# A cached attention head loop with a gated FFN beside it: FFN weights behind the heads, another split of K between VectorE and ScalarE

## The chip, the core and the metric

The kernel runs on one core of one Trainium2 chip. The metric is the device time of one execution in microseconds, as the median over runs. A profile of one execution lies beside it; its times are those of that execution.

## What is computed

One token is decoded. With `xn` the layer norm of `x` (1 x 576), the output is `x + attention(xn) + ffn(xn)`, all in float32:

```python
q = (xn @ wq).reshape(H=32, Dh=128)
scores = einsum("hd,hkd->hk", q, k_cache) * Dh**-0.5     # Sk = 16384 cached keys a head
o = einsum("hk,hkd->hd", softmax(scores), v_cache)
attention = o.reshape(4096) @ wo                          # 4096 -> 576
ffn = (gelu(xn @ w_gate) * (xn @ w_up)) @ w_down          # 576 -> 4608 -> 576
```

The K and V caches are 32 x 16384 x 128 numbers each. Every weight and cache element is read from HBM once: 587.6 MB in all.

## The kernel before

**Slots.** All large loads go through one pool of three SBUF tiles, `slots` (128 partitions x 64 KB). `slot()` takes them in turn; a load into a slot waits until everything that used the slot's last tile is done. Every large load is issued by SyncE (`load`, L60), in program order, so a load that waits holds back those behind it. A K or V load of a head is 8.4 MB, 64 KB a partition: one whole slot.

**Front.** The first slot is `mix`: the last 64 rows of wq, and for gate and up the fourth row of each partition with the last 64 rows. The second is wq. `project` (L121) multiplies the normalized x with a weight on TensorE, four groups of 32 output partitions at a time, and accumulates the steps in PSUM. Q for head h is spread over the partitions by `q_spread` (L143). `ffn` (L153) runs for gate and then up: three more rows of the weight into a new slot, one load each, then the projection, a ScalarE copy into the free end of the same slot (L162), and four small GpSimd copies that lay the result out over 128 partitions in `gu` (L164). So the slot is in use until those copies have landed. `ffn_act` (L171) makes `hT` from `gu` on DVE and ScalarE (tanh).

**Heads.** For each of the 32 heads K and V are loaded (L238, L239). `qk` (L192) works through K in eight blocks of 16 rows a partition: DVE multiplies the block with q in place (L198), ScalarE sums the last 6 rows of each block, one instruction a row with an accumulator that is read by a second instruction (L201), and DVE reduces the other 10 (L202). `softmax` (L204) takes the maximum over all partitions by way of TensorE (L206 to L212) and the exponential on ScalarE (L216). `pv` (L218) multiplies the probabilities with V: 32 matmuls (64 records in the profile) into one PSUM bank, of which only four masked strips are wanted. `out_a` (L225) masks and reduces that bank on DVE (L227, L229), `out_b` (L231) sums it over the partitions on TensorE; for head h - 1 both stand behind block 3 of head h.

**End.** wd (36 rows of 576 numbers a partition) is loaded in pieces of 28 and 8 rows, then wo (32 rows) in pieces of 20, 6, 3, 2 and 1. `add_out` (L255) multiplies one such row with one column of `hT` or `oT`, in two halves; even and odd rows go to different strips of the PSUM tile `acc`. At row `MERGE` of the last weight the two strips are added (L303, L305), and the rows after it go to one strip. Then x is added and the result stored (L309, L310).

The framework places the instructions of one engine in an order of its own where it is not told to keep the program's; the order used here is that of the built program.

Of the kernel before, what the change touches and what calls it, by code (L numbers as in the profile page):

```python
# [10 lines left out]
ALU = mybir.AluOpType  # L11
AX = mybir.AxisListType

P = 128
H, SK, DH = 32, 16384, 128
# [1 line left out]
R = SK // P  # L17
SUB = 16
NSUB = R // SUB
N_ACT = 6  # L20
SLOTS = 3
DJ = 4
DM = P * DJ
# [2 lines left out]
HALF = D // 2  # L26
HD = H * DH
QG, QB = HD // 4, 512
FG, FB = DF // 4, 384
WD_T = DF // P  # L30
WO_T = HD // P
WD_PIECES = (28, 8)
WO_PIECES = (20, 6, 3, 2, 1)
MERGE = 26


@with_exitstack
def kernel(ctx: ExitStack, tc: tile.TileContext, x, k_cache, v_cache, wq, wo, wg, wu, wd, out):
# [18 lines left out]
    def slot():  # L57
        return slots.tile([P, R * DH], F32, tag="s", name="slot")

    def load(dst, src):  # L60
        nc.sync.dma_start(dst, src)
        return dst

    mix, wq_t = slot(), slot()
    at = 0

    def part_of_mix(src):
        nonlocal at
        n = src.shape[1]
        at += n  # L70
        return load(mix[:, at - n : at], src)

    ROW3 = 3 * DF
    tails = {"q": part_of_mix(wtail["q"])}
    load(wq_t, wmain["q"])
    row3 = {}
    for n in "gu":
        row3[n] = part_of_mix(wmain[n][:, ROW3:])
        tails[n] = part_of_mix(wtail[n])

    xrow = cpool.tile([1, D], F32, name="xrow")
    nc.scalar.dma_start(xrow, xf)
# [38 lines left out]
    def project(steps, group, size):  # L121
        pg = ps_big.tile([P, 3, 512], F32, tag="pb", name="pg")
        for k, (j, rhs) in enumerate(steps):
            for b in range(group // size):
                for q in range(4):
                    lo = q * group + b * size
                    if j < DJ:
                        lhs = xnb[:, j, :]
                    else:
                        lhs = xtb[:, q // 2, :]  # L130
                        lo = (q % 2) * group + b * size
                    nc.tensor.matmul(pg[32 * q : 32 * q + 32, b, :size], lhs, rhs[:, lo : lo + size],  # L132
                                     start=k == 0, stop=k == len(steps) - 1)
        return pg[:, : group // size, :size]

    steps = [(DJ, tails["q"])] + [(j, wq_t[:, j * HD : (j + 1) * HD]) for j in range(DJ)]
    pq = project(steps, QG, QB)
    qrow = cpool.tile([P, QG], F32, name="qrow")
    nc.scalar.activation(qrow.rearrange("p (b f) -> p b f", f=QB), pq, AF.Copy)
# [3 lines left out]
    def q_spread(h):  # L143
        r = 32 * (h // (H // 4))
        lo = h % (H // 4) * DH
        pq = ps_s.tile([P, 512], F32, tag="sm", name="pq")
        nc.tensor.matmul(pq[:, :DH], ones[r : r + 1, :], qrow[r : r + 1, lo : lo + DH], start=True, stop=True)  # L147
        Q[h] = spool.tile([P, 1, DH], F32, name="qs")
        nc.scalar.activation(Q[h][:, 0, :], pq[:, :DH], AF.Copy)

    gu = cpool.tile([P, 2, WD_T], F32, name="gu")

    def ffn(which):  # L153
        n = "gu"[which]
        t = slot()
        steps = [(3, row3[n]), (DJ, tails[n])]
        for j in range(DJ - 1):
            lo, hi = j * DF, (j + 1) * DF
            steps.append((j, load(t[:, lo:hi], wmain[n][:, lo:hi])))
        gc = t[:, ROW3 : ROW3 + FG]  # L160
        pg = project(steps, FG, FB)
        nc.scalar.activation(gc.rearrange("p (b f) -> p b f", f=FB), pg, AF.Copy)  # L162
        for q in range(4):
            nc.gpsimd.dma_start(gu[32 * q : 32 * q + 32, which, :], gc[32 * q : 32 * q + 1, :])  # L164

    ffn(0)
    ffn(1)

    hT = cpool.tile([P, WD_T], F32, name="hT")

    def ffn_act():  # L171
        g, u = gu[:, 0], gu[:, 1]
        t1 = cpool.tile([P, WD_T], F32, name="t1")
        nc.vector.tensor_mul(t1, g, g)  # L174
        nc.vector.tensor_scalar(t1, t1, 0.044715, 1.0, op0=ALU.mult, op1=ALU.add)
        nc.vector.tensor_mul(t1, t1, g)
        th = cpool.tile([P, WD_T], F32, name="th")
        nc.scalar.activation(th, t1, AF.Tanh, scale=0.7978845608028654)
        t2 = cpool.tile([P, WD_T], F32, name="t2")
        nc.vector.scalar_tensor_tensor(t2, th, 1.0, g, op0=ALU.add, op1=ALU.mult)  # L180
        nc.vector.scalar_tensor_tensor(hT, t2, 0.5, u, op0=ALU.mult, op1=ALU.mult)  # L181
# [10 lines left out]
    def qk(h, i):  # L192
        kt = KT[h].rearrange("p (n d) -> p n d", d=DH)
        if i == 0:
            S[h] = spool.tile([P, R], F32, name="s")
        lo, nv = i * SUB, SUB - N_ACT
        blk = kt[:, lo : lo + SUB, :]
        nc.vector.tensor_mul(blk, blk, Q[h].to_broadcast([P, SUB, DH]))  # L198
        for n in range(nv, SUB):
            jk = spool.tile([P, DH], F32, name="jk", bufs=1)  # L200
            nc.scalar.activation(jk, blk[:, n, :], AF.Copy, accum_out=S[h][:, lo + n : lo + n + 1])  # L201
        nc.vector.tensor_reduce(S[h][:, lo : lo + nv], blk[:, :nv, :], axis=AX.X, op=ALU.add)  # L202

    def softmax(h):  # L204
        pm = spool.tile([P, 1], F32, name="pm")
        nc.vector.reduce_max(pm, S[h], axis=AX.X)  # L206
        pt = ps_s.tile([P, 512], F32, tag="sm", name="pt")
        nc.tensor.transpose(pt[:1, :P], pm, ident)  # L208
        nm = spool.tile([1, 1], F32, name="nm")
        nc.vector.tensor_reduce(nm, pt[:1, :P], axis=AX.X, op=ALU.max, negate=True)  # L210
        pb = ps_s.tile([P, 512], F32, tag="sm", name="pb")
        nc.tensor.matmul(pb[:, :1], ones[:1, :], nm, start=True, stop=True)  # L212
        nb = spool.tile([P, 1], F32, name="nb")
        nc.scalar.activation(nb, pb[:, :1], AF.Copy, scale=SCALE)  # L214
        PE_[h] = spool.tile([P, R], F32, name="pe")
        nc.scalar.activation(PE_[h], S.pop(h), AF.Exp, bias=nb, scale=SCALE, accum_out=lsum[:, h : h + 1])  # L216
# [8 lines left out]
    def out_a(h):  # L225
        o4 = PO[h % 2].rearrange("p (r d) -> p r d", d=DH)
        tc.keep_in_program_order(nc.vector.tensor_mul(o4, o4, sel.unsqueeze(2).to_broadcast([P, 4, DH])))  # L227
        OM[h] = spool.tile([P, DH], F32, name="om")
        nc.vector.tensor_reduce(OM[h], o4.rearrange("p r d -> p d r"), axis=AX.X, op=ALU.add)  # L229

    def out_b(h):  # L231
        pc = ps_s.tile([P, 512], F32, tag="sm", name="pc")
        nc.tensor.matmul(pc[:, :1], OM.pop(h), ones[:, :1], start=True, stop=True)  # L233
        nc.scalar.activation(oall[:, h : h + 1], pc[:, :1], AF.Copy)  # L234

    q_spread(0)
    for h in range(H):
        KT[h] = load(slot(), kv[h])  # L238
        VT[h] = load(slot(), vv[h])  # L239
        for i in range(NSUB):  # L240
            qk(h, i)
            if h == 0 and i == 3:
                ffn_act()
            if h > 0 and i == 3:
                out_a(h - 1)
                out_b(h - 1)
        KT.pop(h)
        softmax(h)
        if h + 1 < H:
            q_spread(h + 1)  # L250
        pv(h)

    seen = set()
# [5 lines left out]
                             start=q not in seen, stop=last)  # L259
            seen.add(q)  # L260

    wd0, wd1, wo1 = slot(), slot(), slot()
    a, b = WD_PIECES
    n0 = WO_PIECES[0]
    load(wd0[:, : a * D], wdv[:, : a * D])
    load(wd1[:, : b * D], wdv[:, a * D :])
    load(wd1[:, b * D : (b + n0) * D], wov[:, : n0 * D])
    lo = n0
    for n in WO_PIECES[1:]:
        load(wo1[:, (lo - n0) * D : (lo + n - n0) * D], wov[:, lo * D : (lo + n) * D])  # L270
        lo += n
    wd_rows = [wd0[:, j * D : (j + 1) * D] for j in range(a)] + [wd1[:, j * D : (j + 1) * D] for j in range(b)]
    wo_rows = [wd1[:, (b + j) * D : (b + j + 1) * D] for j in range(n0)]
    wo_rows += [wo1[:, j * D : (j + 1) * D] for j in range(WO_T - n0)]

    out_a(H - 1)
    out_b(H - 1)
    pl = ps_s.tile([P, 512], F32, tag="sm", name="pl")
    nc.tensor.matmul(pl[:, :H], ones, lsum, start=True, stop=True)
    rl = cpool.tile([P, H], F32, name="rl")  # L280
# [7 lines left out]
    oT = cpool.tile([P, WO_T], F32, name="oT")  # L288
    nc.gpsimd.dma_start(oT, orow)

    for j, w in enumerate(wd_rows):
        add_out(j % 2, hT[:, j : j + 1], w)

    x2 = wo1[:, R * DH - 2 * HALF : R * DH - HALF]
    nc.vector.memset(x2, 0.0)
    for i in range(2):
        nc.gpsimd.dma_start(x2[32 * i : 32 * i + 1, :], xf[:, i * HALF : (i + 1) * HALF])
    part = wo1[:, R * DH - HALF :]
    nc.vector.memset(part, 0.0)

    for j, w in enumerate(wo_rows):
        if j == MERGE:
            nc.vector.tensor_copy(part[64:], acc[64:, :HALF])  # L303
            for i in range(2):
                nc.tensor.matmul(acc[32 * i : 32 * i + 1, :HALF], ident[:, 64 + 32 * i : 65 + 32 * i], part,  # L305
                                 start=False, stop=False)
        add_out(j % 2 if j < MERGE else 0, oT[:, j : j + 1], w, last=j in (MERGE - 1, WO_T - 1))

    nc.vector.tensor_add(x2[:64], x2[:64], acc[:64, :HALF])  # L309
    nc.sync.dma_start(of.rearrange("o (a f) -> (o a) f", a=2), x2[0:64:32, :])  # L310
# [28 lines left out]
```

## Time and profile before

| | before |
|---|---|
| median of 3 runs (lowest to highest) | 1394.77 us (1393.31 to 1395.02) |
| profiled execution: time, span | 1390.13 us, 1388.4 us |
| DMA | 588.31 MB in 12367 packets, mean 424 GB/s |
| busy share of the span: PE, DVE, ACT | 30%, 71%, 47% |
| one block's DVE multiply (L198), reduce (L202) | 2283 ns, 1477 ns |
| one ScalarE row: ACTIVATE, accumulator read (L201) | 309 ns, 186 ns |
| mean TensorE clock granted | 0.63 |

Times are in microseconds from the start of the span unless marked ns. A line such as `L198` is a line of the kernel before. "A <- B" in a wait means that A waited for B. Queue q1 carries the large loads, q0 the GpSimd copies, q8 and q14 the fetching of the engines' instructions. Beside the views the trace holds each DMA packet with its start, duration, size and queue, but not the DMA engine that moved it; the 4-byte packets at the end of each load are its completion writes.

### The profile page before, as it was taken

To read this page: it belongs to the slowest core of one execution; us is meant where nothing else is said; L and a number is where in the kernel's file an instruction comes from. 1 tells how busy PE (TensorE), PEld (TensorE's weight loads), DVE (VectorE), ACT (ScalarE), POOL (GpSimd) and SP (SyncE) were. 2 spreads that over 40 slices of the span, in tenths; PEclk is the share of its full clock that TensorE was granted. 3 is DMA by queue.
4 is the path that set the end of the run, shared out by engine and by line. 5 is a ranking of instruction groups with operands and counts; after the bars stand their busy time and mean duration, and the time that the engine had idled before them with its cause. 6 is when DMAs were issued, how large, how long until landed. Compare 5 with 4: busy or idle time off the path is not lost.

```text
span 1388.4 us, 10333 instructions
## 1 busy us (share of the span) xinstructions
PE 415.1 (30%) x2881; PEld 113.9 (8%) x2881; DVE 990.0 (71%) x668; ACT 653.6 (47%) x3240; POOL 6.3 (0%) x17
## 2 busy tenths in 40 slices
PE   4511323333332122333231123333321223232317
PEld 1100000000000000000000000000000000000002
DVE  1008888777777887777777887777778887777770
ACT  0105555545454555445445555454545554454450
POOL 0000000000000000000000000000000000000000
PEclk9855565565655556565655665656555565656559
DMA  9999999999999999999999999999999999999996
GB/s 400 431 416 427 439 433 431 435 429 443 427 424 448 423 429 435 423 424 429 431 429 418 433 425 420 431 427 422 427 422 429 434 429 427 427 422 422 424 412 296
DMA packets 12367, 588.31 MB, mean 424 GB/s; under 512 B 1667, under 2 KB 1685, under 8 KB 2070
## 3 DMA queue, kind: packets, MB, share of 16 engines
q1 hardware_dynamic: 11956, 587.60, 98.9%
q8 instruction: 22, 0.36, 0.1%
q14 instruction: 35, 0.29, 0.1%
q0 software_dynamic: 352, 0.06, 0.0%
q10 hardware_dynamic: 2, 0.00, 0.0%
HBM read 587.60 MB, written 0.00 MB: 423 GB/s over the span
## 4 chain that ended last, share of the span: by engine, by line
DMA 49%; DVE 34%; PE 13%; ACT 4%; issue 1%; SPq 0%; POOL 0%; DVEq 0%; ACTq 0%
DMA slot<-in_A_k_cache_dram 41%; DVE slot L198 20%; DVE s L202 11%; PE po L222 10%; DMA slot<-in_B_w_up_dram 3%; ACT jk L201 3%; DMA slot<-in_A_wo_dram 2%; DMA slot<-in_A_wq_dram 2%; DMA gu<-slot 1%; PE pg L132 1%; DVE po L227 1%; DVE om L229 1%; PE acc L258 1%; ACT pe L216 1%; PE pt L208 0%
## 5 line engine op out<-in xcount | busy, mean ns | idle before, releaser
L201 ACT ACTIVATE jk<-slot 128x128 f32<-128x128 f32 x1536 | 475.0, 309 | 552.1 <-DVE slot L198 509.7
L198 DVE TENSOR_TENSOR slot<-slot,qs 128x2048 f32<-128x2048 f32 x256 | 576.4, 2283 | 211.2 <-DMA slot<-in_A_k_cache_dram 211.2
L202 DVE TENSOR_REDUCE s<-slot 128x10 f32<-128x1280 f32 x256 | 370.2, 1477 | 1.1
L222 PE MATMUL po<-slot,pe 128*4 128x512 f32 x2048 | 294.0, 738 | 14.8 <-ACT pe L216 14.5
L201 ACT ACTIVATION_READ_ACCUMULATOR jk<-slot 128x1 f32 x1536 | 286.4, 186 | 0.0
L208 PE MATMUL pt<-ident,pm 128*1 128x128 f32 x32 | 11.9, 373 | 460.9 <-DVE pm L206 460.9
L233 PE MATMUL pc<-ones,om 128*128 128x1 f32 x64 | 18.6, 359 | 438.2 <-DVE om L229 438.2
L222 PEld LDWEIGHTS po<-slot,pe 128*4 128x4 f32 x2048 | 54.5, 98 | 233.8 <-issue 209.7
L233 PEld LDWEIGHTS pc<-ones,om 128*128 128x128 f32 x64 | 15.8, 308 | 467.9 <-DVE om L229 467.9
L174 DVE TENSOR_TENSOR t<-gu 128x36 f32<-128x36 f32 x1 | 0.2, 196 | 65.1 <-DMA gu<-slot 65.1
L132 PE MATMUL pg<-slot,xnb 128*32 128x384 f32 (+1 forms) x256 | 31.5, 643 | 32.6 <-DMA slot<-in_A_wq_dram 13.2
L208 PEld LDWEIGHTS pt<-ident,pm 128*1 128x1 f32 x32 | 2.5, 79 | 464.8 <-DVE pm L206 411.1
L206 DVE TENSOR_REDUCE pm<-s 128x1 f32<-128x128 f32 x32 | 9.1, 286 | 36.7 <-ACT jk L201 36.7
L214 ACT ACTIVATE nb<-pb 128x1 f32<-128x1 f32 x32 | 5.5, 171 | 57.6 <-PE pb L212 57.6
L227 DVE TENSOR_TENSOR po<-po,sel 128x512 f32<-128x512 f32 x32 | 22.0, 688 | 11.3 <-PE po L222 11.3
L147 PE MATMUL pq<-qrow,ones 1*128 1x128 f32 x64 | 24.9, 489 | 0.0
L212 PE MATMUL pb<-nm,ones 1*128 1x1 f32 x64 | 17.7, 343 | 14.8 <-DVE nm L210 14.8
L229 DVE TENSOR_REDUCE om<-po 128x128 f32<-128x512 f32 x32 | 21.8, 682 | 0.0
L181 DVE SCALAR_TENSOR_TENSOR hT<-t,gu 128x36 f32<-128x36 f32 x1 | 0.2, 197 | 28.3 <-DMA gu<-slot 28.3
L210 DVE TENSOR_REDUCE nm<-pt 1x1 f32<-1x128 f32 x32 | 8.9, 279 | 15.0 <-PE pt L208 15.0
L212 PEld LDWEIGHTS pb<-nm,ones 1*128 1x128 f32 x64 | 15.9, 306 | 23.3 <-issue 22.6
L234 ACT ACTIVATE oall<-pc 128x1 f32<-128x1 f32 x32 | 5.5, 171 | 22.6 <-PE pc L233 22.6
(61 smaller groups left out, 116.6 us busy)
## 6 DMA issues: line engine op xcount, KB each, us to landing
slot<-in_B_w_gate_dram SPq DMA_DIRECT2D x4, 2304.0 KB, 44.4
slot<-in_B_w_up_dram SPq DMA_DIRECT2D x4, 2304.0 KB, 35.2
slot<-in_B_w_down_dram SPq DMA_DIRECT2D x1, 8064.0 KB, 35.6
slot<-in_A_wo_dram SPq DMA_DIRECT2D x1, 5760.0 KB, 26.7
slot<-in_B_w_down_dram SPq DMA_DIRECT2D x1, 2304.0 KB, 13.1
slot<-in_A_wo_dram SPq DMA_DIRECT2D x1, 1728.0 KB
slot<-in_B_w_gate_dram SPq DMA_DIRECT2D x1, 1152.0 KB
slot<-in_B_w_up_dram SPq DMA_DIRECT2D x1, 1152.0 KB, 39.4
```

The source lines that it names most:

```text
L132: nc.tensor.matmul(pg[32 * q : 32 * q + 32, b, :size], lhs, rhs[:, lo : lo + size], start=k == 0, stop=k == len(steps) - 1)
L147: nc.tensor.matmul(pq[:, :DH], ones[r : r + 1, :], qrow[r : r + 1, lo : lo + DH], start=True, stop=True)
L198: nc.vector.tensor_mul(blk, blk, Q[h].to_broadcast([P, SUB, DH]))
L201: nc.scalar.activation(jk, blk[:, n, :], AF.Copy, accum_out=S[h][:, lo + n : lo + n + 1])
L202: nc.vector.tensor_reduce(S[h][:, lo : lo + nv], blk[:, :nv, :], axis=AX.X, op=ALU.add)
L208: nc.tensor.transpose(pt[:1, :P], pm, ident)
L212: nc.tensor.matmul(pb[:, :1], ones[:1, :], nm, start=True, stop=True)
L216: nc.scalar.activation(PE_[h], S.pop(h), AF.Exp, bias=nb, scale=SCALE, accum_out=lsum[:, h : h + 1])
L222: nc.tensor.matmul(PO[h % 2][q : q + 4, :], pe[:, k : k + 4], vt[:, k * DH : (k + 4) * DH], start=k < 16, stop=k >= R - 16)
L227: tc.keep_in_program_order(nc.vector.tensor_mul(o4, o4, sel.unsqueeze(2).to_broadcast([P, 4, DH])))
L229: nc.vector.tensor_reduce(OM[h], o4.rearrange("p r d -> p d r"), axis=AX.X, op=ALU.add)
L233: nc.tensor.matmul(pc[:, :1], OM.pop(h), ones[:, :1], start=True, stop=True)
```

## The change

Gate and up leave the front: the first two slots hold wq and its small rest alone, and K of head 0 follows at once in the third. Their loads, projections and `ffn_act` now stand behind the last head, in three slots: three gate rows; a mixed slot with the fourth gate row, the gate tail, the fourth up row, the up tail and the copied gate result; three up rows with the copied up result. Then come wo (28 and 4 rows) and wd (24, 6, 3, 2, 1) in place of wd and then wo; the merge stands at row 30 of wd. ScalarE sums 8 of 16 rows in blocks 0 to 6 of each K and 4 in block 7 (60 a head in place of 48). The masking and reduction of head h - 1 stand behind the softmax of head h; in the built program the one-column product of `out_b` stands behind the first PV matmul of head h, and the first gate matmuls stand ahead of the last head's `out_b`.

```diff
-N_ACT = 6
+N_ACT = (8,) * (NSUB - 1) + (4,)
...
-WD_PIECES = (28, 8)
-WO_PIECES = (20, 6, 3, 2, 1)
-MERGE = 26
+WO_PIECES = (28, 4)
+WD_PIECES = (24, 6, 3, 2, 1)
+MERGE = 30
...
-    mix, wq_t = slot(), slot()
...
+    wq_t, qt = slot(), slot()[:, :QS]
+    load(qt, wtail["q"])
     load(wq_t, wmain["q"])
...
-    def ffn(which):
...
+    def ffn():
+        g, mix, u = slot(), slot(), slot()
+
+        def row(t, at, n, j):
+            return j, load(t[:, at * DF : (at + 1) * DF], wmain[n][:, j * DF : (j + 1) * DF])
+
+        def tail(at, n):
+            return DJ, load(mix[:, at : at + DF // 2], wtail[n])
+
+        steps = [row(g, 0, "g", 0), row(g, 1, "g", 1), row(g, 2, "g", 2), row(mix, 0, "g", 3), tail(2 * DF, "g")]
+        finish(0, project(steps, FG, FB), mix)
+        steps = [row(mix, 1, "u", 3), tail(5 * DF // 2, "u"), row(u, 0, "u", 0), row(u, 1, "u", 1), row(u, 2, "u", 2)]
+        finish(1, project(steps, FG, FB), u)
+
+    def finish(which, pg, t):
+        gc = t[:, 3 * DF : 3 * DF + FG]
         nc.scalar.activation(gc.rearrange("p (b f) -> p b f", f=FB), pg, AF.Copy)
         for q in range(4):
             nc.gpsimd.dma_start(gu[32 * q : 32 * q + 32, which, :], gc[32 * q : 32 * q + 1, :])
-
-    ffn(0)
-    ffn(1)
...
-        lo, nv = i * SUB, SUB - N_ACT
+        lo, nv = i * SUB, SUB - N_ACT[i]
...
         for i in range(NSUB):
             qk(h, i)
-            if h == 0 and i == 3:
-                ffn_act()
-            if h > 0 and i == 3:
-                out_a(h - 1)
-                out_b(h - 1)
         KT.pop(h)
         softmax(h)
+        if h > 0:
+            out_a(h - 1)
         if h + 1 < H:
             q_spread(h + 1)
+        if h > 0:
+            out_b(h - 1)
         pv(h)
...
+    ffn()
+    ffn_act()
...
+    ta, tb, te = slot(), slot(), slot()
+    a, b = WO_PIECES
+    wo_rows = load_rows(ta, 0, wov, 0, a) + load_rows(tb, 0, wov, a, b)
+    wd_rows = load_rows(tb, b, wdv, 0, WD_PIECES[0])
+    lo = WD_PIECES[0]
+    for n in WD_PIECES[1:]:
+        wd_rows += load_rows(te, lo - WD_PIECES[0], wdv, lo, n)
+        lo += n
```

More of the change, by code (lines that the diff above doesn't have):

```diff
@@ L28 @@
 QG, QB = HD // 4, 512
+QS = HD // 2
 FG, FB = DF // 4, 384
@@ L62, in load @@
         return dst
-    mix, wq_t = slot(), slot()
[L65 to L74, printed above, removed]
+    wq_t, qt = slot(), slot()[:, :QS]
+    load(qt, wtail["q"])
     load(wq_t, wmain["q"])
[L76 to L79, printed above, removed]
     xrow = cpool.tile([1, D], F32, name="xrow")
@@ L134, in project @@
         return pg[:, : group // size, :size]
-    steps = [(DJ, tails["q"])] + [(j, wq_t[:, j * HD : (j + 1) * HD]) for j in range(DJ)]
+    steps = [(DJ, qt)] + [(j, wq_t[:, j * HD : (j + 1) * HD]) for j in range(DJ)]
     pq = project(steps, QG, QB)
@@ L151 @@
     gu = cpool.tile([P, 2, WD_T], F32, name="gu")
-    def ffn(which):
[L154 to L161, printed above, removed]
+    def ffn():
[10 more added lines that the diff above has]
+        gc = t[:, 3 * DF : 3 * DF + FG]
         nc.scalar.activation(gc.rearrange("p (b f) -> p b f", f=FB), pg, AF.Copy)
@@ L228, in out_a @@
         OM[h] = spool.tile([P, DH], F32, name="om")
-        nc.vector.tensor_reduce(OM[h], o4.rearrange("p r d -> p d r"), axis=AX.X, op=ALU.add)
+        tc.keep_in_program_order(nc.vector.tensor_reduce(OM[h], o4.rearrange("p r d -> p d r"), axis=AX.X, op=ALU.add))
     def out_b(h):
@@ L260, in add_out @@
             seen.add(q)
[L262 to L274, printed above, removed]
     out_a(H - 1)
@@ L289, with load_rows @@
     nc.gpsimd.dma_start(oT, orow)
-    for j, w in enumerate(wd_rows):
-        add_out(j % 2, hT[:, j : j + 1], w)
-    x2 = wo1[:, R * DH - 2 * HALF : R * DH - HALF]
+    ffn()
+    ffn_act()
+    def load_rows(t, at, src, lo, n):
+        load(t[:, at * D : (at + n) * D], src[:, lo * D : (lo + n) * D])
+        return [t[:, (at + j) * D : (at + j + 1) * D] for j in range(n)]
+    ta, tb, te = slot(), slot(), slot()
[6 more added lines that the diff above has]
+        lo += n
+    x2 = te[:, R * DH - 2 * HALF : R * DH - HALF]
     nc.vector.memset(x2, 0.0)
@@ L297 @@
         nc.gpsimd.dma_start(x2[32 * i : 32 * i + 1, :], xf[:, i * HALF : (i + 1) * HALF])
-    part = wo1[:, R * DH - HALF :]
+    part = te[:, R * DH - HALF :]
     nc.vector.memset(part, 0.0)
     for j, w in enumerate(wo_rows):
+        add_out(j % 2, oT[:, j : j + 1], w)
+    for j, w in enumerate(wd_rows):
         if j == MERGE:
@@ L306 @@
                                  start=False, stop=False)
-        add_out(j % 2 if j < MERGE else 0, oT[:, j : j + 1], w, last=j in (MERGE - 1, WO_T - 1))
+        add_out(j % 2 if j < MERGE else 0, hT[:, j : j + 1], w, last=j in (MERGE - 1, WD_T - 1))
     nc.vector.tensor_add(x2[:64], x2[:64], acc[:64, :HALF])
```

## The prediction

> **What bounds the kernel now.** I read the page's slices and queues first, then rates by stage, then the queue's own waits, then the end of the chain. The page:
>
> ```profile
> span 1388.4 us, 10333 instructions
> ...
> DMA  9999999999999999999999999999999999999996
> ...
> q1 hardware_dynamic: 11956, 587.60, 98.9%
> q8 instruction: 22, 0.36, 0.1%
> q14 instruction: 35, 0.29, 0.1%
> ```
>
> The DMA engines carry packets in every slice; DVE (71%) and ACT (47%) do not. Neither version changes the 587.60 MB, so only three things can move the time: the slowest DMA engine's work, idle time on that engine, and what follows its last byte. Rates by stage (columns: stretch, busy us of each engine, PE clock, DMA share, GB/s):
>
> ```profile
> 76.00:80.00 4.00, 3.77 (x24) 0.99 (x24) 0.00 (x0) 0.00 (x0) 0.00 (x0) 0.50 0.66 279
> 180.00:580.00 400.00, 112.12 (x710) 30.18 (x710) 315.55 (x206) 208.36 (x1041) 0.00 (x0) 0.61 1.00 432
> 580.00:980.00 400.00, 109.70 (x712) 28.60 (x712) 313.02 (x206) 204.92 (x1026) 0.00 (x0) 0.61 1.00 427
> ```
>
> The heads start at 432 GB/s and fall to 427. The trace's packets say why. Each load ends with one 4-byte completion write per engine, 16 in all. At the loads landing from 488.1 to 1315.3 us one write comes last, by 2.5 to 4 us behind the next, and its intervals are of two kinds: 19.35 us (eight 64 KB packets of 2.418 us) or about 20.05. The longer ones hold one of the 8192-byte packets of q14. Such a packet takes 0.309 us and the 64 KB packet after it 2.80 instead of 2.418: 0.69 us together. These fetches come every 128 ACT instructions (every 45.6 us from 435.9 to 1348.9; the kernel has 110.5 ACT instructions a head of 39.4 us), and there are 28 of them. So **one DMA engine carries all of ACT's instruction fetches, and it finishes every load last**. The other 15 run ahead of it until they wait for SP:
>
> ```profile
> SPq L61 <- DVE s L202: 832.8, 32, 28.6
> SPq L61 <- PE po L222: 363.5, 32, 12.2
> SPq L61 <- DMA gu<-slot: 65.3, 2, 36.9
> SPq L61 <- ACT jk L201: 34.9, 32, 1.1
> ```
>
> SP's waits look large, but the slowest engine's shorter interval is exactly its packets: it waits for none of these in the heads. The end of the chain (start, us, what):
>
> ```profile
> 1347.57 26.70 DMA slot<-in_A_wo_dram
> 1374.27 0.14 issue
> 1374.40 6.53 PE acc L258 x104
> 1380.93 0.02 issue
> 1380.96 0.47 DVE slot L303
> ...
> 1382.12 2.93 PE acc L258 x24
> ```
>
> After the 20-row piece of wo lands (1374.27) PE is the limit: 26 rows in 6.53 us, 0.25 a row, on a clock that is already full. The last small piece lands at 1382.04, by its completion write, and does not hold PE up.
>
> **The change, part by part.**
>
> *Sharing of the K blocks.* Before, from the cadence in the chain, a block costs DVE 2.20 (multiply) + 1.39 (10 rows) = 3.59 us. ACT's rows come every 0.433 us. Now DVE needs 2.20 + 0.8 x 1.39 = 3.31 and ACT 8 x 0.433 = 3.46: ACT becomes the longer one. A K tile is released after 2.28 + 7 x 3.46 + 4 x 0.433 = 28.2 us, where it was 31.35 (1315.85 to 1347.20): 3.1 us earlier. That issues the next V load earlier and lets the 15 fast engines run about 3 us further ahead, which is worth nothing while the slowest engine never waits. But ACT gets 12 more rows a head, each an ACTIVATE and a read of its accumulator: 24 x 32 = 768 instructions, 6 more fetches of 128. At 0.69 us each on the slowest engine: **+4.1 us**. Ends: 5 packets of 0.31 alone give 1.6; 7 at 0.76 give 5.3. I take the middle, since 0.69 repeats over the whole run.
>
> *PV mask.* The two DVE operations (0.69 + 0.68 us) go from block 3 to behind the maximum of the next head. They end some 2.5 us after the K tile's last reduce; DVE then waits for K anyway (211.2 us over 31 heads, 6.8 each, and now 3 more). PE's one-column product stands behind the first PV matmul and may hold it 0.5 us; V's slot is needed over 10 us later. Nothing. Without that cover it is 1.4 us a head.
>
> *Gate and up out of the front.* K0's load waited for a slot held by the small gu copies, issued at 73.62; u's last row was through on the first engines at 74.0. The drop to 279 GB/s shows the hole, and 64 KB packets at 74.6 took up to 3.46 us. The engine that later is slowest has writes at 74.3 and 95.0: 20.7 for 19.34, so 1.35 lost; at V1's issue (133.6) another 0.2. Now K0 is issued at once into a free slot; V0 waits until wq is projected (35.1 as before; K0 is through at about 43.5, so 7 us are left after the issue), K1's slot is free by then. **-1.5 us**; ends -0.3 (the gap alone) and -2.7 (all that the fast engines lost).
>
> *Gate and up behind the heads.* With L the landing of K31 on the slowest engine (1315.85 before): g's rows wait for V30 (about L+2, needed L+11 by the fastest engines). The mixed slot waits for K31 (L+28.2; the fastest engines stand about 3 us, the slowest needs it at L+36). u's rows wait for V31 (L+41, needed L+46). wo's 28 rows wait for g's projection (L+48, after PV; needed L+63). The next slot waits for g's gu copies (L+66; 63.2 to 73.47 = 10 us before), needed L+82. The last slot waits for u's gu copies: u lands L+69, one row 4.1, copy 1.1, then 21.0 us as before (81.78 to 102.8), so L+97 with the issue; needed L+101 by the first, L+107 by the slowest engine. POOL does them in order behind the oT copy, long done; ACT's tanh stands ahead of u's copy and waits for g's copies until L+66, covered. Nothing on the slowest engine, with 10 us to spare.
>
> *The tail.* The order ends with wd, and the big piece before the last four is 24 rows instead of 20: 4 x 0.25 = 1.0 us more PE behind it. And PE has been idle: wo's 32 rows are done by about L+98, the 24 rows of wd land about L+107. In the windows the PE clock fell after such pauses:
>
> ```profile
> 1362.00:1366.00 4.00, 3.61 (x37) 1.15 (x41) 0.82 (x4) 0.27 (x1) 1.56 (x3) 0.57 0.99 426
> 1374.00:1378.00 4.00, 3.60 (x60) 1.61 (x64) 0.00 (x0) 0.00 (x0) 0.00 (x0) 1.00 0.89 364
> ```
>
> Before, the idle time ahead of the last rows was 1.5 us and the clock stayed at 1.00. At 0.50 a row takes 0.48. PV bursts stayed slow for 4.1 us (1310.13) to 5.7 (1349.71), the wd rows for 2.7 (1362.71); half of that is lost: 1.35 to 2.85, I take 2.0, the 4.1 row, as its pause was also a cold one. **+3.0 us** with the four rows; ends 1.0 (clock still full) and 3.9. Behind it merge, six rows, addition and store are as before.
>
> Sum: +4.1 - 1.5 + 3.0 = **+5.6 us**. The profiled execution took 1390.13 (span 1388.4 and 1.7 around it), so 1395.7; the median of the runs shown is 4.6 above that execution, so **1400.4**. A change under 0.2% (2.8 us) can't be told from none here.
>
> **Rivals.** *Fetches cost nothing* (17%): if the six fetches fall on engines that run ahead, the sum is -1.5 + 3.0 = +1.5: 1396.3. For it: q14 is 0.1% of the engines' time. Against: the long intervals of the last engine hold its fetches. The Trainium skill ("Trainium Runtime: NRT & Kernel Launch", section on instruction fetch mechanics) says that the sequencer streams its blocks itself and that crossing one is "mostly hidden"; by that rule this rival's time would stand. It is hidden for ACT in this trace, but not for the DMA engine (0.69 us).
>
> *The earlier V issue pays* (11%, faster): SP's late issue starves also the slowest engine, and 3 us more lead ends that. If 427 and 426 GB/s from 580 to 1340 us went back to 432, 324 MB would take 750.3 instead of 760: -9.7 + 1.5 = -8.2, 1386.6. It decides if the last completion write of a load shows gaps in which its engine had nothing queued. For it: 432 falls to 427 just when the lead is used up. Against: 19.35 us is eight packets with no gap.
>
> *The last slot comes late* (7%): if u's gu copies take 42 us instead of 21, the last load is issued 10.8 us too late: 1411.2. It decides above some 31 us. Against: both groups before took 10 and 21 us.
>
> That the new sharing shortens nothing, because ACT becomes the longer engine, alters no time here, as K is released off the slowest engine's path.
>
> **How the numbers follow.** Forecast 65%; with all its lower ends at once (1.6 - 2.7 + 1.0 = -0.1) it gives 1394.7, with all its upper ones (5.3 - 0.3 + 3.9 = 8.9) 1403.7; then 17, 11 and 7. The range 1394.0 to 1404.5 adds 0.7 for the spread of the runs shown (1393.31 to 1395.02); it holds the first two cases and leaves out the last two. Faster 0.11; same 0.19 (the 17% for the most part, and the low end of the forecast); slower 0.70.
>
> **What would show it.** q14 with about 41 packets; the last landing about 2.6 us later; K released 28 us after landing; no drop near 76 us; the clock at 0.5 when wd's 24 rows start and 30 rows in 9 to 10 us. Wrong if q14 stays, if heads run at 432 throughout, if DMA drops near the last slot's issue, or if the clock is 1.0 there.

## The result, and the profile after

The changed kernel takes 1398.54 us in the median of 10 runs (1396.59 to 1399.01); the kernel before, on the same chip, 1394.64 (1391.74 to 1396.32). The ratio is 1.003, 95% interval [1.002, 1.004]: slower by 3.9 us, where +5.6 was predicted. The profiled executions differ more, 1397.76 against 1390.13: the one of before lies 4.5 us under the median of its kernel, the one of after 0.8 under. What is read from that pair has to add up to their own difference in span, 6.5 us, not to 3.9.

The page of after:

```profile
span 1394.9 us, 11109 instructions
...
DMA  9999999999999999999999999999999999999995
...
q1 hardware_dynamic: 11956, 587.60, 98.4%
q8 instruction: 22, 0.36, 0.1%
q14 instruction: 41, 0.34, 0.1%
```

The large loads (q1) and the fetches of q8 are unchanged; q14 has six packets more, as forecast. Rates by stage (stretch, busy us of PE, PEld, DVE, ACT and POOL, PE clock, DMA share, GB/s):

```profile
76.00:80.00 4.00, 3.42 (x20) 0.60 (x24) 0.00 (x0) 0.68 (x4) 0.00 (x0) 0.50 0.93 397
180.00:580.00 400.00, 117.84 (x710) 29.30 (x710) 296.27 (x205) 256.24 (x1275) 0.00 (x0) 0.63 1.00 431
580.00:980.00 400.00, 119.77 (x710) 28.19 (x710) 295.67 (x203) 255.74 (x1273) 0.00 (x0) 0.63 1.00 425
1376.00:1380.00 4.00, 1.52 (x16) 0.56 (x20) 0.00 (x0) 0.00 (x0) 0.00 (x0) 0.50 0.98 398
1380.00:1384.00 4.00, 4.00 (x60) 1.41 (x55) 0.00 (x0) 0.00 (x0) 0.00 (x0) 0.79 0.20 76
```

The drop to 279 GB/s near 76 us is gone (397). The heads lose 1 to 2 GB/s. In the last two rows the clock is 0.50 when the big piece of wd is worked on and full only some 3 us into it. SyncE's waits in its queue (us, times, longest) and the end of the chain (start, us, what):

```profile
SPq L62 <- DVE s L194: 809.6, 32, 36.7
SPq L62 <- PE po L214: 407.3, 32, 13.6
SPq L62 <- DMA gu<-slot: 38.8, 3, 20.5
SPq L62 <- ACT jk L193: 33.2, 32, 1.1
```

```profile
1338.58 39.76 DMA slot<-in_B_w_down_dram
1378.34 0.14 issue
1378.48 9.05 PE acc L249 x120
1387.53 0.02 issue
1387.55 0.47 DVE slot L296
1388.03 0.04 issue
1388.07 0.65 PE acc L298 x4
1388.72 2.94 PE acc L249 x24
```

The 6.5 us, followed by the completion writes of the slowest DMA engine: K of head 0 landed at 95.1 us before and lands at 43.9 now. That is 51.2 earlier, of which 49.65 are the packets of gate and up, now behind the heads: the front saves 1.6. From there to V of head 30 it was 1200.2 and is 1205.7: +5.5. From that V, with K and V of head 31 still to come, to the landing of the last big piece, it was 78.97 and is 128.74 - 49.65 = 79.09: +0.1. The rows behind that landing: 9.05 against 6.53 us: +2.5. Sum +6.5; merge, last rows and store are as they were.

The 5.5 can be taken apart. The trace does not name a packet's DMA engine, but the packets that end in the last completion write of V of head 30 can be followed back to K of head 0, as each starts within 0.02 us of the end of the one before. In both executions this chain of packets has no gap: 488 packets of 64 KB, and between them 26 fetches before and 32 now. The fetches, each with what the packet behind it takes over 2.418 us, come to 17.0 and 21.0 us, 0.65 each: +4.0. The rest is nearly all in other 64 KB packets that took over 2.45 us: their excess is 3.5 us before and 4.9 now.

### The profile page after: what moved, and what is told of

It is laid out like the page before. It is cut to its first block, busy times and chain, and to the rows that moved or that the text cites. A ratio compares the mean times of both kernels' runs of the same rounds, so it can differ in the third digit from the quotient of the medians.

```text
span 1394.9 us, 11109 instructions
## 1 busy us (share of the span) xinstructions
PE 442.6 (32%) x2881; PEld 113.9 (8%) x2881; DVE 939.3 (67%) x668; ACT 811.2 (58%) x4008; POOL 6.3 (0%) x17
## 4 chain that ended last, share of the span: by engine, by line
DMA 49%; ACT 28%; PE 16%; DVE 3%; issue 3%; POOL 0%; SPq 0%; DVEq 0%
DMA slot<-in_A_k_cache_dram 44%; ACT jk L193 27%; PE po L214 12%; DMA slot<-in_B_w_down_dram 3%; DVE slot L190 3%; DMA slot<-in_A_wq_dram 2%; PE pg L120 1%; PE acc L249 1%; DMA gu<-slot 1%; PE pc L225 1%; ACT pe L208 1%; PE pb L204 0%; PE pt L200 0%; DVE pm L198 0%; DVE nm L202 0%
## 5 line engine op out<-in xcount | busy, mean ns | idle before, releaser
L193 ACT ACTIVATE jk<-slot 128x128 f32<-128x128 f32 x1920 | 594.1, 309 | 331.6 <-DVE slot L190 272.1
L193 ACT ACTIVATION_READ_ACCUMULATOR jk<-slot 128x1 f32 x1920 | 357.4, 186 | 0.0
L214 PE MATMUL po<-slot,pe 128*4 128x512 f32 x2048 | 324.0, 692 | 16.2 <-ACT pe L208 16.2
L194 DVE TENSOR_REDUCE s<-slot 128x8 f32<-128x1024 f32 (+1 forms) x256 | 316.5, 1278 | 0.0
L204 PE MATMUL pb<-nm,ones 1*128 1x1 f32 x64 | 17.6, 342 | 14.8 <-DVE nm L202 14.8
L127 ACT ACTIVATE qrow<-pg 128x1024 f32<-128x1024 f32 x1 | 1.0, 1024 | 30.7 <-PE pg L120 30.7
```

Of the source, the lines that this page charges most:

```text
L214: nc.tensor.matmul(PO[h % 2][q : q + 4, :], pe[:, k : k + 4], vt[:, k * DH : (k + 4) * DH], start=k < 16, stop=k >= R - 16)
```

## Experiments

Two theories. The first is the prediction's: the heads last as long as one DMA engine needs, the one that carries ACT's instruction fetches at 0.69 us each, so the 12 extra ACT rows a head are what costs. The second: fetches cost little, and the rest does it, by the order at the end with its cold clock, by the moved masking, or by K released earlier. The table has the difference of each run's median to that of the kernel before on the same chip in the same series of runs; the ratio is taken over all their runs, so the two can differ by about a us.

| run | base | q14 packets | to before, us | ratio, 95% interval |
|---|---|---|---|---|
| after | | 41 | +3.9 | 1.003 [1.002, 1.004] |
| e1 new sharing alone | before | 41 | +4.7 | 1.0037 [1.0024, 1.005] |
| e2 more ACT instructions | before | 41 | +1.3 | 1.001 [0.9999, 1.0021] |
| e3 more DVE instructions | before | 41 | -3.2 | 0.9985 [0.9974, 0.9995] |
| e4 old sharing | after | 35 | -1.4 | 0.9992 [0.9984, 1.0001] |
| e5 wd in small pieces | after | 41 | +1.1 | 1.0004 [0.9994, 1.0013] |
| e6 two ACT rows | after | 19 | -13.3 | 0.99 [0.9888, 0.9912] |
| e7 two rows and small pieces | after | 19 | -15.4 | 0.9887 [0.9873, 0.99] |
| e8 masking moved alone | before | 35 | +1.0 | 1.0002 [0.9992, 1.0012] |
| e9 gate's slot freed in the front | before | 35 | -1.1 | 0.9993 [0.9983, 1.0002] |
| e10 K released late | after | 53 | +13.2 | 1.0096 [1.0082, 1.011] |
| e11 one ACT row, small pieces | after | 15 | -10.6 | 0.992 [0.9905, 0.9935] |
| e12 PE kept warm | after | 41 | +3.5 | 1.0023 [1.0014, 1.0032] |

**The sharing, alone and undone.** e1 puts only the new sharing into the kernel before; e4 takes only it out of the kernel after.

```diff
-N_ACT = 6
+N_ACT = (8,) * (NSUB - 1) + (4,)
...
-        lo, nv = i * SUB, SUB - N_ACT
+        lo, nv = i * SUB, SUB - N_ACT[i]
```

> The kernel before with the new split of K alone (8 ScalarE rows in blocks 0 to 6, 4 in block 7). Fetch theory: 768 more ScalarE instructions, 6 more q14 packets (41), the last load lands 4.1 us later (up to 5.4 if the restarts of the other engines add to it), nothing else moves: 1394.6 + 4.1 to 5.4 = 1398.7 to 1400.0. Rival, the heads go by when K's slot is freed: it is freed some 2 us earlier, so the time stays or falls, 1394.6 or less. Rival, the whole loss lies behind the last head: 1394.6.

```diff
-N_ACT = (8,) * (NSUB - 1) + (4,)
+N_ACT = (6,) * NSUB
```

> The changed kernel with 6 ScalarE rows in every block. Fetch theory: q14 back to 35 packets, the last load 4.1 to 5.4 us earlier than in the changed kernel, its end as slow as there: 1398.5 - 4.1 to 5.4 = 1393.1 to 1394.4; against the kernel before it shows the front (-1.5 forecast) and the end (+2.5) alone. Rival, the loss lies behind the last head: 1398.5. Rival, K's slot: freed 3 us later than in the changed kernel, 1398.5 or more.

e1 took 1398.93, +4.7. e4 took 1392.87, -1.4. The two add up (+4.7 - 1.4 = +3.3 for the +3.9 of the whole change): the sharing is what makes the kernel slower, and the rest together is worth about nothing or a small gain. The end of the chain points the same way: the rows of the last big piece start at 1380.73 in e1 and at 1373.37 in e4:

```profile
1380.73 8.24 PE acc L258 x104
```

```profile
1330.68 42.56 DMA slot<-in_B_w_down_dram
1373.24 0.14 issue
1373.37 10.15 PE acc L249 x120
```

The line of e1 holds something else: its 104 records, the same 26 rows that took 6.53 us in the profiled execution of before, took 8.24.

**Instructions without work.** e2 and e3 add tiny instructions to each block of the kernel before, on ACT (1024 copies and 224 waits fewer, so 800 more in all) and on DVE (768).

```diff
+        for _ in range(4):
+            nc.scalar.activation(tiny, blk[:, nv, :1], AF.Copy)
```

> The kernel before, split as before, with four one-element ScalarE copies a block whose result nobody reads: 1024 instructions, 224 waits fewer, 800 more in all. Fetch theory: 6 more q14 packets (41), the last load 4.1 us later: 1398.7. Rival, K's slot: ScalarE has over 1 us to spare in a block of 3.59, K is freed at most 0.7 us later, and the fast DMA engines run 5 us ahead: 1394.6. Rival, the loss lies behind the last head: 1394.6.

```diff
+        for _ in range(3):
+            nc.vector.tensor_copy(tiny, blk[:, 0, :1])
```

> The kernel before with three one-element VectorE copies a block that nobody reads (768 instructions). Fetch theory: about 6 more q14 packets, but on the DMA engine that carries VectorE's fetches, which runs ahead of the slowest one: 1394.6 within 1 us, although K is freed 2 to 3 us later. Rival, any instruction fetched costs the same: 1398.7. Rival, K's slot: it is freed 2 to 3 us later in every head, 1394.6 plus up to 64 to 96.

The page of e3, its queue line and its new group:

```profile
q14 instruction: 41, 0.34, 0.1%
...
L201 DVE COPY tiny<-slot 128x1 f32<-128x1 f32 x768 | 114.6, 149 | 6.8
```

DVE's fetches fall into q14 too, six more, and the time does not rise: -3.2. So six packets on that queue are not the price by themselves; whose they are counts. Followed back as above, the packets of the engine that lands last hold 26 fetches in e3, as in before, so DVE's six went through other engines. That the run is 3.2 us faster, where 0 within 1 us was expected, has no shown cause; K is released later here (the next V load issued 32.85 us after the first K multiply, median over the heads, 31.34 before). e2 gives less than expected: in its profiled execution the rows of the last big piece start at 1378.70, 4.3 later than before, and the chain of packets holds 31 fetches, but the median of 12 runs is only +1.3, with an interval from -0.1 to +2.9. So the one experiment that adds ACT's fetches and little else does not show 4.1 us in its runs. Its runs and those of before in that series both spread over 5.9 us; why they fall short of the profile stays open.

**Fewer ACT rows.** The strongest test of the theory is the other direction: two ACT rows a block, 16 a head for 60.

```diff
-N_ACT = (8,) * (NSUB - 1) + (4,)
+N_ACT = (2,) * NSUB
```

> The changed kernel with only 2 ScalarE rows in each block (14 on VectorE). Fetch theory: 16 instead of 60 rows a head, 2816 ScalarE instructions less, 22 fetches less on the slowest DMA engine at 0.69: up to -15.2, so 1383.3, with q14 at 19; less if another engine is then slowest. VectorE needs 8 x 4.15 = 33.2 us for a K and 36 with its other steps, under the 38.7 us of two loads. Rival, K's slot: it is freed 5 us later than in the changed kernel, 1398.5 or more.

The page, the heads by stage, and the end of the chain:

```profile
span 1377.6 us, 8293 instructions
...
q14 instruction: 19, 0.16, 0.0%
```

```profile
180.00:580.00 400.00, 119.42 (x710) 29.45 (x710) 360.64 (x206) 77.05 (x382) 0.00 (x0) 0.63 1.00 432
580.00:980.00 400.00, 122.23 (x727) 29.36 (x731) 356.11 (x208) 76.44 (x379) 0.00 (x0) 0.63 1.00 431
```

```profile
1360.70 0.14 issue
1360.83 9.39 PE acc L249 x120
```

The second 400 us now run at 431 GB/s (425 after, 427 before) with the same bytes, although DVE has become the busier engine (356 us of these 400, 296 after). Against before it is -13.3 us, against after -17.2 (each taken to the kernel before of its series). Landing of the big piece: 1378.34 to 1360.70, -17.6 for 22 fetches fewer, where 22 x 0.69 = 15.2 is the price read from the trace of before. Followed back as above, the engine that lands last has 11 fetches in e6 where after has 32: 7.5 us against 21.0. That is 13.5 of the 17.4 by which K of head 0 to V of head 30 got shorter; another 4.6 is gone from the other long packets (4.9 after, 0.35 here), and the short ones take a little more. The median 64 KB packet of that engine takes 2.42 us in before, after and e6 alike, with ACT busy for 47%, 58% and 18% of the span, so it is not ACT's work as such that slows the loads. K is released late here too (33.18), but that alone is not it: e3 has 32.85 and gains 3.2.

**The rest of the change.** e8 moves only the masking, as the change does; e9 frees the slot that K of head 0 waited for, in the kernel before.

```diff
-            if h > 0 and i == 3:
-                out_a(h - 1)
-                out_b(h - 1)
...
+        if h > 0:
+            out_a(h - 1)
...
+        if h > 0:
+            out_b(h - 1)
```

> The kernel before with only the PV mask and reduction moved behind the next head's softmax. Theory: VectorE waits for K anyway and the slowest DMA engine's packets stay the same, 0 within 1 us of the kernel before (K is freed 1.4 us earlier, which lets the fast engines run further ahead and may cost the slowest one up to 0.7). Rival, K's slot: freed 1.4 us earlier in 31 heads, up to 43 us less. Rival, uncovered VectorE work: 1.4 us a head more.

```diff
-        gc = t[:, ROW3 : ROW3 + FG]
+        gc = t[:, ROW3 : ROW3 + FG] if which else mix[:, :FG]
```

> The kernel before with gate's copied result put into the mixed slot, over the wq rows that are used up, so that the load of K0 no longer waits for gate's small copies and is issued some 12 us earlier. If the hole near 76 us costs what the profiled execution shows, 1.35 us less: 1393.3. If it is larger in most executions (the kernel before spreads over 6 us, the changed one over 2.4), up to 4 us less and a smaller spread. Rival, the front is hidden anyway: 1394.6.

e8: +1.0, interval from -1.1 to +1.7: no effect that can be measured, although V's load is issued 2.2 us earlier (29.15). e9: -1.1, from -2.4 to +0.3, which fits the 1.5 taken for the front but does not establish it. Its windows show one hole gone and another at V1's issue (131.06), where before has 393 GB/s in the same 4 us:

```profile
76.00:80.00 4.00, 3.50 (x24) 0.94 (x24) 0.20 (x1) 0.11 (x1) 0.00 (x0) 0.64 1.14 492
130.00:134.00 4.00, 1.98 (x9) 1.11 (x13) 1.32 (x3) 1.85 (x10) 0.00 (x0) 0.50 0.78 295
```

**The tail.** e12 keeps PE busy between the rows of wo and wd with nine matmuls whose result nobody uses; e5 loads the first 24 rows of wd in three pieces, so that most rows are done before the last of them lands.

```diff
+    dm = ps_s.tile([P, 512], F32, tag="sm", name="dm")
+    for k in range(9):
+        nc.tensor.matmul(dm, ident, ta[:, k * 512 : k * 512 + 512], start=True, stop=True)
```

> The changed kernel with nine matmuls on wo's rows into an unread PSUM tile between the last wo row and the first wd row, so that TensorE is busy until about a microsecond before wd's 24 rows land. Theory of the tail: the clock is then full and 30 rows take 7.5 us in place of 9.05 to 10.15 (three executions), so 1.5 to 2.6 us less: 1395.9 to 1397.0. Rival, the clock plays no part: 1398.5, or more if the added matmuls hold the rows up.

```diff
-WD_PIECES = (24, 6, 3, 2, 1)
+WD_PIECES = (8, 8, 8, 6, 3, 2, 1)
```

> The changed kernel with wd's 24-row piece loaded as three of 8 rows (8, 8, 8, 6, 3, 2, 1). The DMA side stays (last landing 8.4 us after the third piece). Theory of the tail (PE is late behind the big piece: 9.05 us for 30 rows, half of it at a halved clock): only 14 rows are left when the third piece lands, 3.5 us at full clock and 6.7 at half, so the merge comes 2.4 to 5.5 us earlier: 1398.5 - 2.4 to 5.5 = 1393.0 to 1396.1. Rival, the last landing sets the end: 1398.5.

Windows and chain of e12:

```profile
1376.00:1380.00 4.00, 2.82 (x14) 1.00 (x16) 0.00 (x0) 0.00 (x0) 0.00 (x0) 1.00 0.96 400
1380.00:1384.00 4.00, 4.00 (x76) 1.70 (x68) 0.00 (x0) 0.00 (x0) 0.00 (x0) 1.00 0.49 195
```

```profile
1379.61 7.50 PE acc L249 x120
```

The clock is 1.00 where after has 0.50 and 0.79, and 30 rows take 7.50 us, 0.25 each, for 9.05: the cold clock cost 1.55 us in the profiled execution of after. The timing is less clear: 1396.14 lies in the expected range, but before was 2.0 lower in that series, and by the ratios (1.0023 against 1.003) the gain is 1.0 us with overlapping intervals. e5 gains more: +1.1 to before, where after is at +3.9 (its profiled execution, 1396.35, is the slowest of its runs and is not read here). Put on top of e6 the same pieces give e7, 1377.27 us against 1379.36:

> Both at once: 2 ScalarE rows a block and wd's 24 rows in three pieces. The two act in different places, so the gains add: 1383.3 less 2.4 to 5.5 = 1377.8 to 1380.9 by the fetch theory and the theory of the tail. By the rivals 1398.5 or more.

The gains add as expected, the time lying just under the expected range. e7 is the best kernel here, 0.9887 of before [0.9873, 0.99] and 1377.27 against 1398.54 of after. Its diff is that of e6 and e5 together.

**How late may K be released?** In the sums of the heads something remained that is not fetches. With 0.69 us for each fetch taken off, the slowest engine needs more than its own packets by this much, beside the time of the V issue after the first K multiply:

| run | V issue, us | remainder, us |
|---|---|---|
| e6 | 33.18 | 0.8 |
| e3 | 32.85 | 0.9 |
| before | 31.34 | 2.4 |
| e4 | 29.15 | 2.8 |
| e8 | 29.15 | 3.7 |
| e1 | 28.9 | 4.0 |
| after | 28.34 | 3.6 |

In these seven runs the remainder rises, though not evenly, the earlier the other 15 engines get new work. By the same sum e7 (33.18) has 1.1, e2 (31.37) 2.7, and e5 and e12, with the heads and the V issue of after, 4.5: so about 0.9 is the spread between executions. The packets show where the time goes. Most of the slowest engine's long 64 KB packets without a fetch before them start within 9 us behind V's issue, when the waiting engines get new work. In after they took up to 3.2 us; the excess of those packets is 4.6 us there, 3.3 in before and 0.3 in e6. But in e3, which issues V almost as late as e6, it is 3.0; its small remainder comes from fetches at 0.61 us each, where the table takes 0.69. So the loss begins at V's issue, and how much it is does not follow from the time of the issue alone. To move that time alone, e10 delays K's release in the kernel after by six tiny DVE copies a block.

```diff
+        for _ in range(6):
+            nc.vector.tensor_copy(tiny, blk[:, 0, :1])
```

> The changed kernel with six one-element VectorE copies a block that read K and that nobody reads, so that K's slot is freed 3 to 5 us later and the fast DMA engines run less far ahead; ScalarE's fetches stay (34 of them), VectorE's rise by 12 on another engine. If running ahead costs the slowest engine (what is left of its intervals after the fetches is 0.8 us in the heads where V is issued at 33 us, 2.4 at 31, 3.6 at 28), the last load lands 1.2 to 2.8 us earlier than in the changed kernel: 1395.7 to 1397.3. If the lead is free: 1398.5. Rival, K's slot: 1398.5 plus up to 100 to 150.

It overshot. (The twelve packets more in q14 are fetches of the 1536 copies.) V was issued at 35.85 and the run is +13.2 us; the first and last completion writes of a load lie only 2 us apart (8 to 10 after), so hardly an engine is ahead when K's slot comes free. The waits of its queue name who holds it:

```profile
SPq L62 <- DVE tiny L193: 1086.6, 32, 44.8
SPq L62 <- PE po L217: 169.2, 32, 6.1
```

This tells where the release becomes the bound, not whether an early one costs. e11 closes in from the other side, with one ACT row a block and the pieces of e5:

```diff
-N_ACT = (8,) * (NSUB - 1) + (4,)
+N_ACT = (1,) * NSUB
```

> One ScalarE row a block, wd's 24 rows in three pieces. Fetch theory with only the slowest engine counted: 512 instructions less than with two rows, 4 fetches, -2.8: 1374.5. With the other engines counted: at two rows the last engine was only 0.5 to 1.4 us behind the next, so no more than about 1 us less, 1376.3 to 1377.3, and the bound has moved to other engines. Rival, VectorE becomes the bound (8 x 4.29 + 3 = 37.3 us a head against 38.7): above 1378.

Its q14 has 15 packets, four fewer than e7, and it is slower, 1382.07 against 1377.27. DVE's reduces are now 15 rows long:

```profile
L194 DVE TENSOR_REDUCE s<-slot 128x15 f32<-128x1920 f32 x256 | 538.1, 2143 | 0.0
```

V is issued at 34.25 us. The fetch theory's 1374.5, or 1376.3 to 1377.3 with the other engines counted, did not come; the rival named there, VectorE as the bound (above 1378), fits: VectorE's longer blocks set when K is released. So between 33.2 (e6) and 34.3 (e11) K's release seems to take over as the bound. Two ACT rows a block is the best of the sharings tried.

## Why the prediction was right, and where it was off

- **Direction and bound: right.** One DMA engine with ACT's fetches sets the pace of the heads: its packets run without a gap, with 26, 32 and 11 fetches in before, after and e6. The times of e1 (+4.7) and e6 (-17.2 against after) go with it; the runs of e2 (+1.3) show less than its fetches should cost. q14 went to 41 packets as forecast. One reading was too narrow: from 488.1 to 1315.3 us the last write of a load lies 1.8 to 4.6 us behind the next, not 2.5 to 4; it is always the last, so the argument holds.
- **Six fetches, +4.1: too small for the sharing as a whole.** The heads of the profiled execution grew by 5.5, e1 by 4.7, and the last landing came 4.2 us later in place of 2.6 (1382.04 to 1386.27). The fetches themselves were sized right in the profiled pair: +4.0, at 0.65 each and not 0.69. What the term left out is the long packets behind V's issue, +1.4. The step that failed is "worth nothing while the slowest engine never waits": it never waits, but its packets get longer when the others start again. That this grows with the lead is only argued from the table above; e10 could not show it, and e8, with 29.15, shows no time that can be measured.
- **Front, -1.5:** 1.6 by the completion writes, and the drop is gone.
- **PV mask, 0:** as forecast (e8).
- **Gate and up behind the heads, 0:** right (+0.1). The copies of u took 14.7 us (1345.57 to 1360.26) and not 21, so more was spare than assumed. The next V load is issued 28.34 us after the first K multiply (28.2 forecast).
- **Tail, +3.0: the mis-sized term of the forecast for the median.** In the profiled pair it is +2.5: the clock was 0.50 as forecast and the 30 rows took 9.05 us, at the short end of 9 to 10. But the 6.53 us of before that it was counted from was a favourable case. In the profiled executions of e1, e2, e3, e8 and e9, all with the tail of before, the same 104 records took 8.06 to 8.24. There PE had stood idle for 2.9 to 6.6 us ahead of these rows and the clock was 0.50 for 3.1 to 3.5 us at or near their start; in the execution of before the pause was 1.5 us and the clock stayed full. Against their mean of 8.19 the term is +0.9 for after and +1.2 for the mean of after, e4, e6 and e10 (9.43). With +4.7 (e1) and -1.6 that makes +4.0 to +4.3, and +3.9 was measured; this sum was made up afterwards and mixes medians with profiled executions. So the claim of the tail step that the clock stayed at full speed before held for the execution read and not for the kernel, and adding a difference of profiled executions to a median carried that luck over: +5.6 forecast, +3.9 measured. That the forecast came as near as this is luck in part: the sharing was counted too low and the tail too high, and the two partly cancel. The chains of e3 and e9:

```profile
1372.99 8.22 PE acc L261 x104
```

```profile
1374.43 8.06 PE acc L258 x104
```

- **Rival "fetches cost nothing":** its 1396.3 is only 2.2 us under the measured median, so the time alone would not have told it from the forecast. The packets exclude it: all six more fetches stand in the chain of the engine that lands last. e6 goes with that: a gain of 17 us with 22 fetches fewer, while ACT and DVE both had idle time in after. The Trainium skill ("Runtime: NRT & Kernel Launch", section "Instruction fetch mechanics") calls the crossing of an instruction block "mostly hidden". The trace of before agrees for ACT itself (within a block no two rows start more than 0.82 us apart, in the median 0.434), and not for the DMA engine, where a fetch costs 0.65 us in this kernel bound by DMA.
- **Rival "earlier V issue pays":** excluded; the heads fell to 425 GB/s and e1 and e8 gain nothing.
- **Rival "last slot late":** excluded by the 14.7 us, with a DMA share of 1.03 in the 4 us from 1360, where that load is issued.

## What to carry to other kernels

In a kernel bound by DMA as this one is, follow the last of a load's 16 completion writes: here the slowest engine, not the mean rate, set the time, and what else went through that engine lengthened it. Work shared between two compute engines is then to be shared with an eye on the number of instructions as well as on time: two ScalarE rows a block in place of eight (four in the last block) made this kernel 17 us faster although VectorE got the longer share, up to the point where the slot came free too late. And before a term is counted from a profiled execution, see where that execution stands in the spread of its kernel: here it was 4.5 us under the median, and 1.7 of it lay in one burst of matmuls.

## What the runs showed of the hardware

- Which engine's instructions are fetched decides, not their number: six more packets in q14 stand in the chain of the slowest DMA engine when they are ACT's (26 fetches before, 32 in e1 and after) and not when they are DVE's (26 in e3). The medians are +4.7 us (e1, with the new sharing), +1.3 (e2, ACT copies alone) and -3.2 (e3).
- The same 26 rows took 6.53 us in one execution, behind a pause of 1.5 us and with the clock at 1.00, and 8.06 to 8.24 in five others, behind pauses of 2.9 to 6.6 us and with the clock at 0.50 for some 3 us. The Trainium skill ("TensorE: Matmul & The Clock Gate", Part 1) says that the window over which activity is counted runs freely and the start of the full clock varies from run to run. These numbers do not test that, as the pauses differ too. Nine idle matmuls ahead of the rows kept the clock at 1.00 (e12).
- The distance between the first and the last completion write of a load stops growing at 5 to 7 us before and at 8 to 10 with K released 3 us earlier, as if the fast engines then run out of issued work.
